# A fused attention and two-layer expert kernel: norm factors turned in 32-wide blocks and stored as rows, one factor of seven kept as half a place, and a new order table

## The chip, the cores and the metric

The kernel runs on one core of a Trainium2 chip. The metric is device microseconds of one execution, as the median over runs. Before the change the median of three runs is 1045.04 us (1044.8 to 1048.22).

## The reference, cut to what matters

```python
# q, k, v: (4 batches, 12 heads, 448 tokens, 64); S = 448
scores = q @ k.T / sqrt(64) - log(S)
attn   = 1 / (1 + exp(-scores))
x      = (attn @ v) -> (1792 tokens, 768)
# first layer: d_ff = 1536
rms = sqrt(mean(x * x, axis=-1) + 1e-06)
xn  = x / rms * rms_g
g   = xn @ w_gate
x   = (g * sigmoid(g) * (xn @ w_val)) @ w_out
# second layer: d_ff = 2048
h   = x @ w_in
out = (h - tanh(h)) @ w_out2
```

All values are 32-bit floats, and the products are made from rounded high parts and remainders of their factors.

## The kernel before

**Stages.** The four batches are worked as two groups of two, (0, 1) and (2, 3). For each of the 48 heads the scores of a head are made on TensorE with keys on the partitions (L750, and L771 for the last 64 keys), put through the sigmoid on ScalarE (L759) and multiplied with the values (`pair_av` L807, `tail_av` L791) into one PSUM bank per pair of heads. VectorE or ScalarE copies the bank to SBUF (`copy` L437). The six pairs of a batch give x with the 768 features on six times 128 partitions and the 448 tokens along the free axis. ScalarE squares the six parts and VectorE adds them (L830), which leaves one 128 x 448 tile of partial sums of squares.

**The norm.** `norm(b)` (L836 to L853) then needs, for each of the 448 tokens, the sum over 128 partitions. TensorE makes it with four products (L842) whose weights are 112 tokens of the tile and whose moving operand is a column of ones. They add into a PSUM bank that a VectorE memset (L845) has set to zero; that memset has no input, and it is the first instruction of VectorE's queue for batch 0. VectorE scales the 112 x 4 sums (`ms`, L847), GpSimd raises them to the power -0.5 (`rc`, L849), and SP stores the 112 x 4 factors to DRAM in token order with one DMA whose elements are 4 bytes (L852). `spread_norm` (L857) loads the 448 factors back to all 128 partitions, and VectorE multiplies x by them and by `rms_g` (`x_whole`, L923).

**The layers.** From about 127 us on, the two layers run. They are products of blocks in the seven-product scheme: four blocks of a weight matrix are combined into seven factors, and sums of x are combined the same way. `raw` tiles hold 128 rows of a weight matrix (L485); VectorE and ScalarE split each into a rounded part and a remainder (L437, L508, L519) and combine blocks (L572, L604). The factors of a weight pass are kept in DRAM for the second group of batches: `keep` stores them (`put` L586) and `again` loads them back (L634 to L637). A place of a stored factor is 128 x 768; the fourth one, A22, fills half of it, and is stored and loaded at full size.

**What sets the order.** All work is recorded first as pieces with an engine, a duration and dependences. `Plan.lay` then gives out the pieces to the queues of five engines; where several could go, the rank of each piece in the table `ORDER` decides (a base-64 text of some 5,000 numbers, one per piece). The queues run in order, so a piece that waits holds all pieces behind it on its engine. SP issues most loads, the norm's stores and the reloads of factors; GpSimd issues loads of values and of `raw` weights and the stores of factors.

**The start.** While the first inputs land, TensorE makes `N_WARM` = 6 products of zeros (`whole_bank` L442, weights and moving operand are the tile `mark`). `mark` is set to zero by GpSimd (L1223), behind its memset of `zero` (L478).

Of the kernel before, what the change touches and what calls it, by code (L numbers as in the profile page):

```python
# [9 lines left out]
F32 = mybir.dt.float32  # L10
# [5 lines left out]
AF = mybir.ActivationFunctionType  # L16
# [6 lines left out]
P = 128  # L23
# [14 lines left out]
N_WARM = 6  # L38
# [202 lines left out]
a2f03b00003b0mT04X04u08F0Ly03c0000OB0000000Cc0Xd0cta3v0K10aW0o203b0We1s61l_1pz5dA0Lo2jB0Za12m0gb0O92Ng17A18y1aQ19b3hi05l  # L241
0fA1ex0000Ho0Z20OX0nZ1F905j1bI2Fk0kb2R20KR1hz4zf0Ei1w20000000b20000dI0Op1GO1nR20i0O_1_l2Qd37T2hh3_E59j46I5TC1Dw0gP00H1IT
01e0ED0001Qu0000E_0Xx0001yz0ON0Xg1T-0_j2NP1a52VS15E2C13ZD00Q3TH3oy1oG3Cj2wN06cAJ72uw36U3D70IX1Sc6gY3Kk2-y5ug3N92tf0f22Db
3Ob6Z74122YZ3412_B3FW3HR2ZM3tp3Il26j4MJ6JS4Qx2XT3Rn3O21gW2ge3fl1i42Z52JX2Tu21a1x_2Jx3Ud3x12Rq2IT27N2cI2E92G62qU2Fn2QJ2fF
2t239K4Wx3Fm4Rz3x42Fd2hO1a21fk1_S1hX0vE21H1ON18s1B52jj1-K2gX1ZZ1Oc1ku3Br3oO1w71fE1s_1ar1iv2T41fy1Dn0xa1s_1XP0Fl0Fl0za0_B
0uV2Ty2Sf2SB1FT2Jj1Nz0sM2SW3zX3Gd1-A1M61yz1Kh2HV1IT1xo2Tj1U_2NH27314T1If2Dm1th1ld1lM1zT1Wa58K3UK1q22Jy1w02oL1ig0dx0EF0Cf
0EN0GT0eR0mf0pk1f12R41u01-Z0Dm14a1jx3oQ1MU1P70Cf1W50wx1hu0Cf1WR0Qc1-91Xl0qw1Tb2CH2aq2Vy0Cf80P3H81bb2k_1W224h1w_1O_1Iz0fu
0Cf0VV0Cf0Cf0tD0in0L00PJ0_r1OQ0U10Et1tX2F13451uq2AP1tn1bZ1lk0_D11V0cd14k1Jy0Cf0ak1R51EP0ug28W1kZ0Cf0IV1jo1w22TF17H0sZ18W
17x2NQ34m1XD2Z727o1qk2pT1oe3OW2dN2lJ2Dr2Ry3Tx1gY1ab1Kp1nC2511VM1U-2Wl1Xb1bn2W01qB1aJ1Kn0Vr3g23ik3FR1_o0zg1tL1aR1TX1-P0-I
1uk1Kz1W22nz1qh2ko19G1JY20x2Ns1RL3Ow1-T2oq2SP2G72Kt2r-2ML2YF3ik2BJ1sV2Sn2VM2LQ2KR23w2DH2Pt2dK36s1J71nF2Dw2Jd1vt2UC1YS1tw  # L250
2FW1nQ2n_1yh2tU3H240-0vl1sG2YR4jm2Ah3VR4De30C2Tf35m32P2cv28m1mK1Pv0I65A63Kq0dN3UI3Bi1-H2hk2nW2Kz41222z2BY07N34o0M42oM33P
3Bm2Og1Oi1QU0EZ2RG2b93pV21g1W21w_0kw3Rn3kr4Og0mu25Q1-P2qv1qn5Gt37Z49R2_G3-J1kW2nZ3Hm22M3FG3NL2bR0Cf5Mv2pr34V3m03xb2Fq2Qp
3Dq1_16Bf2Mn0DJ2kq2IJ1m22YZ2as2b835w2Vv3uj5VQ1h109e5610WT3o13c92843_t1oL64O54k3mw3BY3JU42a3LY39U2gM1tJ2Q43bs5eE61739o2dJ
2a73ml49V1-p3-X3wE2C13nB4Fc2eO1Yt5u96az2XW3t337B6QH5Q64qs56h2KU2pC2K-2ZA6zp6Uk2g03hH4sY7oM2-c3W_5CB2-12q_24x4Fk3JP2KJ0VS
6K71Ak6jG4ke5Wj1FA3Cf3bA3fG6GS3aB2mv20l2qp3pO3Dn3no3_83063U62gT1wa1gf3Le1Hz2AL2XK1es2In1nb2de4Pe2zc2AE2Q21iP1rM1K31ao0fW
2rw0wN3lV1FV0tZ21k2Sj2-o1EL2_x25b1wx4Tw4kJ0002BI2gz2mP2XU0Dt3O60DE5JL1QT3293RF4XA05L3nV3Ll1eQ4GR51033G2pf4_J4tx32W4Ut2Gx
3xm2o-2ru3P83zW4Lp3DD3LQ34U3j65Fx0SD54O55a4BN4xo3WM7gh6yv3Ls3fa0OV6H_6Ty7-R2rk02U5bi3be1aU72C8EC4qa6SX6NICG62TE3_p22Y4JA
5Gu0KF6w24HV3KY4OI4js2ck2M_4Xd1IH5Ht7y5AHq5Ob4J14O17IW2tc5AX6jU4vx6F16_73YX6zw6K661Z1i75sV6uP64t7Bm8Oe3vU00q9ZI6P70000up
09N9zp6s47wL3BV7T06q08Ng50B74C025000DqM6Ka6EJ6039LT6rR9gI8xP8jp7OG6ppC9k6j068X7cvA9C7BGBNS2hDBpT2je30b3TbHhkGT58326ff7rH
83D6TFCFxBlC4sr8Ui7Cx67M60G6zq9i23BS9Jj6qK6w08Qc8NxAJk7hy7gDA8Y6DLCxC6R06nz8mG9se7sm5yI1155q15wnCaY0aF0Nm7QZDFA6Ag5dB7Fg  # L260
BAR1o68G66zL6Eu82S85O6X16rF9l0CFW18TApRDeCDKHBSsBEmDCXE5zFAM4-w79sAdD95X90BC8cBlb9226d279j6bU9T-7SK6B5A8Z7c16CK6fCAYC7rM
# [102 lines left out]
def tile_sigmoid_attention_moe_moe(  # L364
# [233 lines left out]
    def pair_units(ph, i, rs, j):  # L598
# [787 lines left out]
```

## Time and profile before

| | |
|---|---|
| median of 3 runs | 1045.04 us (1044.8 to 1048.22) |
| the profiled execution: its own time | 1050.69 us |
| its span on the core | 1048.9 us |
| mean granted clock of TensorE | 0.989 |
| busy: TensorE, its weight loads, VectorE, ScalarE, GpSimd | 98%, 84%, 75%, 64%, 15% |
| DMA | 247.11 MB, mean 236 GB/s |

The profiled execution is 5.65 us above the median of the runs, and 1.8 us of it lie outside the span. A line of the timeline is a run of like instructions: its start, how long it lasts from the first to the last, the engine, the line of the kernel, the operation and its tiles, a count, and in brackets the idle time of the engine before it and what ended it. L437 is the line of a helper that copies and casts for many places, so its tile names tell which copy it is.

### The profile page before, as it was taken

To read this page: it belongs to the slowest core of one execution; us is meant where nothing else is said; L and a number is where in the kernel's file an instruction comes from. 1 tells how busy PE (TensorE), PEld (TensorE's weight loads), DVE (VectorE), ACT (ScalarE), POOL (GpSimd) and SP (SyncE) were. 2 spreads that over 40 slices of the span, in tenths; PEclk is the share of its full clock that TensorE was granted. 3 is DMA by queue.
4 is the path that set the end of the run, shared out by engine and by line. 5 is a ranking of instruction groups with operands and counts; after the bars stand their busy time and mean duration, and the time that the engine had idled before them with its cause. 6 is when DMAs were issued, how large, how long until landed. Compare 5 with 4: busy or idle time off the path is not lost.

```text
span 1048.9 us, 15266 instructions
## 1 busy us (share of the span) xinstructions
PE 1024.1 (98%) x5258; PEld 881.1 (84%) x5258; DVE 788.5 (75%) x1274; ACT 675.9 (64%) x1233; POOL 161.4 (15%) x218
## 2 busy tenths in 40 slices
PE   9898999899999999999999999999999999999998
PEld 4454459799999888899999989999998999999997
DVE  5575889797965985886865867899886878676766
ACT  6575875675764655675664756778675767665742
POOL 4431110000013032111003030000303210003030
PEclk9898999999999999999999999999999999999999
DMA  8789868958649879969759589287969882849493
GB/s 312 276 279 248 311 217 247 297 189 305 222 138 288 317 167 317 364 196 405 283 159 234 190 232 289 78 306 265 216 206 219 275 214 76 268 113 222 123 227 132
DMA packets 99117, 247.11 MB, mean 236 GB/s; under 512 B 13184, under 2 KB 52032, under 8 KB 99040
## 3 DMA queue, kind: packets, MB, share of 16 engines
q1 hardware_dynamic: 74384, 178.23, 50.9%
q0 software_dynamic: 24512, 67.84, 26.2%
q8 instruction: 41, 0.67, 0.3%
q14 instruction: 36, 0.29, 0.1%
q10 hardware_dynamic: 144, 0.07, 0.0%
HBM read 152.90 MB, written 93.20 MB: 235 GB/s over the span
## 4 chain that ended last, share of the span: by engine, by line
PE 67%; issue 13%; DMA 11%; DVE 5%; POOL 3%; ACT 2%; SPq 0%; POOLq 0%; DVEq 0%; ACTq 0%
PE ps L1125 33%; PE ps L1070 22%; PE ps L1150 5%; PE ps L807 3%; DMA wAg<-part 3%; DMA wD<-part 2%; PE ps L750 2%; DMA raw<-in_w_out 2%; POOL out L948 1%; DMA part<-wB 1%; DVE part L519 1%; DMA out<-unit 1%; DMA rc<-rc 1%; DMA unit<-rc 1%; DVE part L508 1%
## 5 line engine op out<-in xcount | busy, mean ns | idle before, releaser
L1125 PE MATMUL ps<-unit,part 128*128 128x448 f32 x2520 | 524.4, 366 | 11.8 <-ACT unit L437 6.0
L1125 PEld LDWEIGHTS ps<-unit,part 128*128 128x128 f32 x2520 | 473.5, 189 | 57.3 <-ACT unit L437 9.5
L1070 PE MATMUL ps<-unit,part 128*128 128x448 f32 x1512 | 311.4, 364 | 0.0
L1070 PEld LDWEIGHTS ps<-unit,part 128*128 128x128 f32 x1512 | 283.5, 187 | 22.3
L519 DVE TENSOR_TENSOR part<-part 128x768 fp32r<-128x768 f32 (+1 forms) x244 | 215.1, 891 | 77.7 <-ACT part L437 54.5
L437 ACT COPY unit<-ps 128x448 f32<-128x448 f32 x292 | 151.6, 535 | 117.0 <-PE ps L1070 45.6
L437 ACT CAST part<-part 128x768 fp32r<-128x768 f32 (+1 forms) x236 | 183.4, 787 | 41.8 <-DMA part<-wB 8.1
L877 DVE TENSOR_TENSOR unit<-unit 128x448 fp32r<-128x448 f32 x252 | 153.1, 620 | 38.6 <-ACT unit L437 23.4
L437 ACT CAST unit<-unit 128x448 fp32r<-128x448 f32 x260 | 144.1, 570 | 48.0 <-DVE unit L989 24.1
L1006 DVE TENSOR_TENSOR unit<-ps,unit 128x448 f32<-128x448 f32 x168 | 103.2, 622 | 46.3 <-PE ps L1125 18.6
L759 ACT ACTIVATE unit<-ps 128x448 f32<-128x448 f32 x168 | 79.7, 571 | 31.8 <-PE ps L750 22.7
L882 DVE TENSOR_TENSOR unit<-unit 128x448 f32<-128x448 f32 x144 | 86.5, 619 | 7.5 <-DMA unit<-sumB 3.9
L948 POOL DMA_DIRECT2D sumB<-unit x48 | 41.6, 942 | 261.1 <-DVE unit L1006 165.6
L508 DVE SCALAR_TENSOR_TENSOR part<-raw,zero 128x768 uint32<-128x768 uint32 x68 | 64.8, 953 | 10.4 <-ACT zero L437 8.6
L437 ACT CAST zero<-raw 128x768 f16<-128x768 bf16 x52 | 56.2, 1080 | 18.6 <-DMA raw<-in_w_val 6.9
L807 PE MATMUL ps<-unit,part 128*64 128x448 f32 x288 | 62.4, 569 | 2.9 <-DVE unit L437 2.9
L1150 PE MATMUL ps<-unit,part 128*128 128x448 f32 x288 | 60.3, 365 | 0.5
L1150 PEld LDWEIGHTS ps<-unit,part 128*128 128x128 f32 x288 | 53.7, 187 | 6.1 <-DVE unit L934 1.0
L948 POOL DMA_DIRECT2D out<-unit x36 | 30.7, 964 | 177.3 <-DVE unit L1006 168.3
L750 PEld LDWEIGHTS ps<-unit 64*128 64x128 f32 x396 | 37.6, 193 | 18.2 <-ACT unit L759 7.7
L750 PE MATMUL ps<-unit 64*128 64x448 f32 x396 | 49.8, 390 | 0.0
L604 DVE TENSOR_TENSOR part<-part 128x384 f32<-128x384 f32 x80 | 43.2, 552 | 8.6 <-DMA wAg<-part 7.5
(52 smaller groups left out, 475.1 us busy)
## 6 DMA issues: line engine op xcount, KB each, us to landing
raw<-in_w_out POOLq DMA_DIRECT2D x28, 768.0 KB, 9.0
part<-wD SPq DMA_DIRECT2D x56, 384.0 KB, 5.1
part<-wB SPq DMA_DIRECT2D x36, 384.0 KB, 5.9
wC<-part SPq DMA_DIRECT2D x36, 384.0 KB, 4.2
part<-wC SPq DMA_DIRECT2D x36, 384.0 KB, 4.5
raw<-in_w_in SPq DMA_DIRECT2D x16, 768.0 KB, 6.2
sumB<-unit POOLq DMA_DIRECT2D x48, 224.0 KB, 8.1
wD<-part POOLq DMA_DIRECT2D x28, 384.0 KB, 7.1
```

The costliest lines, as they stand in the source:

```text
L437: add(engines, lambda e: (nc.scalar.copy if e == "ACT" else nc.vector.tensor_copy)(to(), of()), reads, writes)
L519: add({**dve(n, psum=False), **pool(n)}, lambda e: ENG[e].tensor_sub(lo(), of(), hi().bitcast(F32)), [*reads, *kh], [*kl])
L750: nc.tensor.matmul(ps[i].tile[:, :S], lhsT=k_of(w, b, c, i), rhs=x.tile[rows, :S], start=q == 0, stop=q == len(terms) - 1)
L759: add(act(S, psum=True), lambda e: nc.scalar.activation(to.tile, ps.tile[:, :S], AF.Sigmoid, bias=-math.log(S), scale=1.0 / math.sqrt(D)), ...
L807: nc.tensor.matmul(ps.tile[HEADS[i], :S], lhsT=v_of(v, b, c, i), rhs=a[c][i].tile, start=opens and c == 0, stop=not opens and c == MAIN - ...
L877: add({**pool(S), **dve(S, psum=False)}, lambda e: ENG[e].tensor_sub(t["l"].tile, of.tile, t["h"].tile.bitcast(F32)), [of["t"], kh], [kl])
L882: add({**dve(S, psum=False), **pool(S)}, lambda e: ENG[e].tensor_sub(t.tile, x.tile, y.tile), [x["t"], y["t"]], [t["t"]])
L948: add(queue("POOL", True), lambda e: nc.gpsimd.dma_start(out=d.tile, in_=t.tile, accum_op=ALU.add), [t["t"], d["t"]], [d["t"]], moved=move ...
L1006: add(dve(S), lambda e: nc.vector.tensor_add(t.tile, ps.tile[:, :S], t.tile), [ps["t"], t["t"]], [t["t"]])
L1070: nc.tensor.matmul(ps.tile[:, :S], lhsT=part(a), rhs=x[b].tile, start=n in (1, 5) and kp == 0 and q == 0, stop=kp == n_kp - 1 and q == 2, ...
L1125: nc.tensor.matmul(ps.tile[:, :S], lhsT=part(a), rhs=x[b].tile, start=n in ((1, 2, 5) if opening else (1, 5)) and i == 0 and q == 0, stop= ...
L1150: nc.tensor.matmul(ps.tile[:, :S], lhsT=wt, rhs=a[p].tile, start=start and i == 0, stop=stop and i == 2, skip_group_check=True)
```

## The change

- `norm(b)` works on blocks of 128 tokens (128, 128, 128 and 64). Its memset of the PSUM bank now reads the finished squares, so the bank is given out only behind them. The factors go into the first 4 columns of a 128 x 32 tile of zeros (a new VectorE memset), VectorE transposes that tile in blocks of 32 x 32 (a new instruction), and each of the four groups of 32 partitions then holds four rows of 32 factors. SP stores them with four DMAs of four rows of 128 bytes, in place of one DMA with 448 elements of 4 bytes. The load behind it is of the same size as before, and waits for all four.
- The pool of the norm's small tiles has four buffers instead of two.
- The fourth factor is stored as its 384 columns and loaded as these. There are 18 such stores and 18 such loads, of 192 KB in place of 384 KB.
- `mark` is set to zero by VectorE as its first instruction, and there are nine products of zeros.
- In `plain_units` the first 12 products of a list, not 8, are sorted by their weight block.
- `ORDER` is wholly new.

```diff
-N_WARM = 6
+N_WARM = 9
 ORDER = """
-a2f03b00003b0mT04X04u08F0Ly03c0000OB0000000Cc0Xd0cta3v0K10aW0o203b0We1s61l_1pz5dA0Lo2jB0Za12m0gb0O92Ng17A18y1aQ19b3hi05l
+qV906300005U03D00z06306306300F00006306O0K719d3BQ7HAqXR4Ru1pO8lK2h_3jv05U6XF2fm1_S6JE2LN0Xw4q40xP42i5Jf5Wm6dX48k24T0002qQ
...
-    norm_p = ctx.enter_context(tc.tile_pool(name="norm", bufs=2))
+    norm_p = ctx.enter_context(tc.tile_pool(name="norm", bufs=4))
...
     mark = const.tile([P, S], BF16, name="mark")
+    nc.vector.memset(mark, 0.0)
...
-    expo = const.tile([TK, 4], F32, name="expo")
+    expo = const.tile([P, 4], F32, name="expo")
...
             if (ph, i) not in SPLIT:
-                put(d, at, x)
+                if at < 3:
+                    put(d, at, x)
+                else:
+                    add(queue("SP"), lambda e: nc.sync.dma_start(out=d.tile[:, at, :NH].rearrange("p (k c) -> p k c", c=P), in_=one_of(x.tile, 1)),
+                        [x[1]], [d[at]], moved=moved(4 * P, 3 * P))
                 return
...
-    def again(d, at):
+    def again(d, at, n=NW):
         w = part_of("again", [P, NW])
-        add(queue("SP"), lambda e: nc.sync.dma_start(out=w.tile, in_=d.tile[:, at]), [d[at]], [w[0], w[1]], moved=moved(4 * NW))
+        add(queue("SP"), lambda e: nc.sync.dma_start(out=w.tile[:, :n], in_=d.tile[:, at, :n]), [d[at]], [w[0], w[1]], moved=moved(4 * n))
...
     def norm(b):
-        ms, rc = (Slot(None, lambda t=t: norm_p.tile([TK, 4], F32, tag=t, name=t)) for t in ("ms", "rc"))
+        ms, rc, rt = (Slot(None, lambda t=t, n=n: norm_p.tile([P, n], F32, tag=t, name=t)) for t, n in (("ms", 4), ("rc", 32), ("rt", 32)))
         def sums(e):
             for i in range(4):
+                n = min(P, S - i * P)
                 nc.tensor.matmul(
-                    ps.tile[:TK, i:i + 1], lhsT=sq.tile[:, i * TK:(i + 1) * TK], rhs=ones[:, 0:1], start=False, stop=True, skip_group_check=True)
-        add({"DVE": (130, False)}, lambda e: nc.vector.memset(ps.tile[:TK, :4], 0.0), [], [ps["t"]])
+                    ps.tile[:n, i:i + 1], lhsT=sq.tile[:, i * P:i * P + n], rhs=ones[:, 0:1], start=False, stop=True, skip_group_check=True)
+        add({"DVE": (130, False)}, lambda e: nc.vector.memset(ps.tile[:, :4], 0.0), [sq["t"]], [ps["t"]])
...
-        add({"POOL": (2100, True)}, lambda e: nc.gpsimd.tensor_tensor(out=rc.tile, in0=ms.tile, in1=expo, op=ALU.pow),
-            [ms["t"]], [rc["t"]])
-        d = rcs[b] = Slot(None, lambda: dram_p.tile([4, TK], F32, name=f"rc{b}"))
-        add(queue("SP"), lambda e: nc.sync.dma_start(out=d.tile.rearrange("i t -> t i"), in_=rc.tile), [rc["t"]], [d["t"]], moved=moved(4, S))
+        add({"DVE": (130, False)}, lambda e: nc.vector.memset(rc.tile, 0.0), [], [rc["t"]])
+        add({"POOL": (2100, True)}, lambda e: nc.gpsimd.tensor_tensor(out=rc.tile[:, :4], in0=ms.tile, in1=expo, op=ALU.pow),
+            [ms["t"], rc["t"]], [rc["t"]])
+        add({"DVE": (180, False)}, lambda e: nc.vector.transpose(rt.tile, rc.tile), [rc["t"]], [rt["t"]])
+        d = rcs[b] = Slot(None, lambda: dram_p.tile([4, 4, 32], F32, name=f"rc{b}"))
+        for k in range(4):
+            add(queue("SP"), lambda e, k=k: nc.sync.dma_start(out=d.tile[:, k], in_=rt.tile[32 * k:32 * k + 4]), [rt["t"]], [d[k]], moved=300)
...
-        order = sorted(order[:8], key=lambda x: x[1]) + order[8:]
+        order = sorted(order[:12], key=lambda x: x[1]) + order[12:]
...
-    nc.gpsimd.memset(mark, 0.0)
     nc.gpsimd.memset(ones, 1.0)
```

**VectorE, about 35 us into the kernel** (`zero<-raw` is the first step of splitting a raw weight tile, `unit<-ps` is the copy that frees the PSUM bank of a pair of heads, `unit<-part` and `unit<-part,unit` round q or k and take the remainder). Before, and then in the change, whose line numbers are a few higher:

```order
33 L437 CAST zero<-raw 128x768
34 L830 TENSOR_TENSOR unit<-unit 128x448
35 L508 SCALAR_TENSOR_TENSOR part<-raw,zero 128x768
36 L437 COPY unit<-ps 128x448
37 L437 CAST unit<-part 128x384
38 L572 TENSOR_TENSOR part<-part 128x768
```

```order
33 L438 CAST zero<-raw 128x768
34 L510 SCALAR_TENSOR_TENSOR part<-raw,zero 128x768
35 L836 TENSOR_TENSOR unit<-unit 128x448
36 L574 TENSOR_TENSOR part<-part 128x768
37 L438 CAST unit<-part 128x384
38 L438 COPY unit<-ps 128x448
```

The copy that frees the bank stays behind the cast of the same raw tile, with two more pieces between them. Since the norm no longer holds a bank from the start, the piece of TensorE that needs this copy comes one step later in TensorE's queue: the scores of the next head, not the `pair_av` before them.

**TensorE, the attention of the first group** (L842, now L849, are the norm's sums; L791 and L771, now L797 and L777, the tails that end a pair of pairs). Before, up to the sums of batch 0, and then the change up to the same sums:

```order
39 L750 MATMUL ps<-unit 128x448 x18
40 L807 MATMUL ps<-unit,part 64x448 x6
41 L750 MATMUL ps<-unit 128x448 x18
42 L807 MATMUL ps<-unit,part 64x448 x6
43 L771 MATMUL ps<-part 64x448 x4
44 L791 MATMUL ps<-unit,part 64x448 x4
45 L842 MATMUL ps<-ones,unit 112x1 x4
```

```order
37 L777 MATMUL ps<-part 64x448 x4
38 L797 MATMUL ps<-unit,part 64x448 x4
39 L756 MATMUL ps<-unit 128x448 x18
40 L813 MATMUL ps<-unit,part 64x448 x6
41 L849 MATMUL ps<-ones,unit 128x1 x3
42 L849 MATMUL ps<-ones,unit 64x1
43 L756 MATMUL ps<-unit 128x448 x18
```

The sums of batch 0 come six rows earlier: behind the row that ran at 50.99 us before. Those of batch 1 stay where they were, behind the last tail of their batch.

**SP, the store and the reload of the factors of batch 0** (`rc_1058` and `rc_803` are the DRAM tiles of the factors, `in_qkt` and `in_vt` the inputs of later heads). Before, and then in the change:

```order
28 L691 DMA part<-in_qkt 128x448 x4
29 L691 DMA part<-in_vt 128x2x256 x2
30 L852 DMA rc_1058<-rc 112x4x1
31 L691 DMA part<-in_qkt 128x448 x3
32 L857 DMA unit<-rc_1058 128x448
33 L691 DMA part<-in_qkt 128x448
```

```order
26 L697 DMA part<-in_qkt 128x448
27 L862 DMA rc_803<-rt 4x32
28 L697 DMA part<-in_qkt 128x448 x2
29 L697 DMA part<-in_vt 128x2x256 x2
30 L697 DMA part<-in_qkt 128x448 x2
31 L862 DMA rc_803<-rt 4x32 x3
32 L697 DMA part<-in_qkt 128x448 x4
33 L697 DMA part<-in_vt 128x2x256 x2
34 L867 DMA unit<-rc_803 128x448
```

Four short stores stand in place of one, the first a few loads earlier in the queue, and eight to thirteen other issues lie between a store and the reload where there were three.

At the start of VectorE's queue the cast of the first raw weight tile, which stood behind two rounded inputs (rows 2 and 4) and in front of the third (row 7), now stands in front of the second.

## Rows read from the trace of the kernel before

**Rows 1.** The page, part 1 and the clock of part 2.
```profile
PE 1024.1 (98%) x5258; PEld 881.1 (84%) x5258; DVE 788.5 (75%) x1274; ACT 675.9 (64%) x1233; POOL 161.4 (15%) x218
PEclk9898999999999999999999999999999999999999
```
**Rows 2.** TensorE's waits: line, releaser, total us, times, longest.
```profile
PE ps L1125 <- ACT unit L437: 6.0, 4, 3.3
PE ps L842 <- DVE unit L830: 3.8, 2, 3.4
```
**Rows 3.** TensorE's timeline: start, us, instructions, [idle before <- releaser].
```profile
1.94 2.42 PE L444 MATMUL ps<-mark 128*128 128x448 bf16 x6 [1.94 <-POOL mark L1223]
4.29 5.86 PE L750 MATMUL ps<-part 64*128 64x448 f32 x24
...
11.00 2.48 PE L807 MATMUL ps<-unit,part 128*64 128x448 f32 x12
13.40 2.09 PE L750 MATMUL ps<-unit 64*128 64x448 f32 x18
...
37.55 4.75 PE L807 MATMUL ps<-unit,part 128*64 128x448 f32 x12 [2.90 <-DVE unit L437]
42.23 2.71 PE L750 MATMUL ps<-unit 64*128 64x448 f32 x18
...
53.40 0.87 PE L750 MATMUL ps<-unit 64*128 64x448 f32 x6
```
**Rows 4.** TensorE's timeline at the sums of batch 1.
```profile
95.38 1.65 PE L842 MATMUL ps<-ones,unit 128*112 128x1 f32 x8 [3.42 <-DVE unit L830]
96.97 3.73 PE L750 MATMUL ps<-unit 64*128 64x448 f32 x18
```
**Rows 5.** TensorE's timeline in the layers: three of its ten later waits.
```profile
200.05 5.26 PE L1125 MATMUL ps<-unit,part 128*128 128x448 f32 x17 [3.31 <-ACT unit L437]
417.15 3.90 PE L1125 MATMUL ps<-unit,part 128*128 128x448 f32 x18 [1.48 <-ACT unit L437]
804.22 8.10 PE L1125 MATMUL ps<-unit,part 128*128 128x448 f32 x31 [2.50 <-ACT ps L437]
```
**Rows 6.** Windows: busy us per engine (count), granted clock, DMA share, GB/s.
```profile
95.00:105.00 10.00, 9.62 (x52) 6.77 (x54) 7.14 (x14) 5.54 (x13) 3.46 (x5) 0.67 0.92 173
130.00:160.00 30.00, 30.00 (x182) 16.91 (x179) 26.99 (x49) 22.82 (x49) 6.25 (x1) 1.00 0.67 221
160.00:195.00 35.00, 34.99 (x178) 32.09 (x177) 31.25 (x53) 19.21 (x29) 1.31 (x1) 1.00 0.91 239
```
**Rows 7.** VectorE's timeline: the raw tiles' casts at 14 and 35 us.
```profile
14.62 0.62 DVE L437 CAST zero<-raw 128x768 f16<-128x768 bf16 x1 [4.25 <-DMA raw<-in_w_out]
...
34.99 0.60 DVE L437 CAST zero<-raw 128x768 f16<-128x768 bf16 x1 [6.74 <-DMA raw<-in_w_out]
...
36.88 0.62 DVE L437 COPY unit<-ps 128x448 f32<-128x448 f32 x1
```
**Rows 8.** SP's and VectorE's timelines: store, reload and use of batch 0's factors.
```profile
74.85 0.34 SPq L852 DMA_DIRECT2D rc<-rc  x1
82.43 0.33 SPq L857 DMA_DIRECT2D unit<-rc  x1
90.89 1.28 DVE L923 SCALAR_TENSOR_TENSOR unit<-unit,g_sb 128x448 f32<-128x448 f32 x2 [4.35 <-DMA unit<-rc]
```
**Rows 9.** DMA, 175 to 202 us in 40 slices, and its issues there.
```profile
GB/s 451 419 387 423 414 414 387 352 127 391 414 387 396 305 246 259 250 346 410 360 292 259 86 50 14 77 109 132 141 191 137 210 241 414 423 414 319 414 396 419
part<-wB SPq DMA_DIRECT2D x4, 384.0 KB, 11.2
rc<-rc SPq DMA_DIRECT2D x1, 1.8 KB, 14.1
```
**Rows 10.** DMA, 72 to 86 us: its GB/s in 40 slices.
```profile
GB/s 362 383 435 421 343 424 356 375 386 263 136 30 53 39 17 23 23 16 26 51 164 119 96 137 124 146 88 97 61 103 124 94 167 240 252 353 433 420 460 404
```
**Rows 11.** The page, part 6: median us from issue to landing.
```profile
part<-wB SPq DMA_DIRECT2D x36, 384.0 KB, 5.9
```

More of the change, by code (lines that the diff above doesn't have):

```diff
@@ L245 @@
[L245 to L249, printed above, removed]
@@ L355 @@
[L355 to L359 removed]
+qV906300005U03D00z06306306300O00006306O0K719d3BQ7HAqXR4Ru1pO8lK2h_3jv05U6XF2fm1_S6JE2LN0Xw4q40xP42i5Jf5Wm6dX48k24T0002qQ
@@ new lines @@
+06319M3MC3TG06T28D2ks0631pa2Xg0BS3ix2hx0J52izEM77Ea5B803S03S9M40631Ye4xF03S03S78z2ym11D6SN2HU4-f9JIAk0CF6CUf0pK0hK02t5lv
+0001zv0005Ca03S1Ki9iL0Cr2b507D2fyA1Z5E38oHCQl6mi28r5IB7010PX7_F6396C09RZ2r90Lxbvm8Yv8QjFsA1UO3VBH9t6T970qHWs6u55910a00dt
+8EOE1c77E8Qm6QE2M12OV4VvAws8GyBA08JZBXbF0QEkx4UN7XQC0e1ne3ltBsj2ZG4CK5qO4SP4sP2uU2Ow9m-BR_5gN2g43bb3UB1zC3uM5Bv3pb3-y2Fg
+2zn2ZU5fM7Lu9LSBC672y4ss0WM24q3fM0n70DR5fq0IM1G233P3oh48l3l61M_1do2Cr89Q96_0uM16r2S522A3HH1yx3Ou3Pf29E2f34LM2Do37L2k52Cr
+2_y3fn48I3B61Oe4Pg2xM0kg3iv4fn3h42Gn14W3CM2cp3Zw3wM45d41K4BD4AF4QI2GK2u62h_1wT41k4J61gB2g94vR4vM1J43Tf3sS4aY1-l56T1-M12j
@@ new lines @@
+3hI0dw1Hx1pZ2FZ3ky3gy2Iy1oi1rH2tX1JA5912Mt2lT2r13G80xf02v3Z_37B0S43IB1rE0R32vN5Ae49D4p-3BP6184MVNGI5NB3hZ8ZS1ri1M94P_2i0
+2o_33O3sX32b29L18k1Py1Kf3Vz2Ux2PE3he0_l3Bv2OB2u81l034i2o92Xj3P22Au2AU2mq1n91uv07m0mV2Gx1Rx24y2pH0zp1cc0QE2m63lw1KL33Y0n1
+2J34dY2x22fg11V14E2845Lx12n3mr3RK3D35PL3Wv4qC4Oy6DU2hU5KQ4-92Sc3Fh0tO4Db3uN1Va4SY3fT3Sz2uz3e51Ox1nS3Na2nW5M37oH2_Y3ky2Lz
+2YU35b1vK3u83FE2B22l33Nz63u4ZS56n3lO2hT4S_5gk3-d5P25IR5U943P0i45TW5r97OX5Eh3Pq3XA2YK5dv0gg4et2pX7pi0QV4Gz3ek4Cs3IC2Hu5b9
+4zu5KT4TC4Rp1Ry1oL4nH37734N3fh2iy4nD3oi5tk3dh4Ob7aV4a44wb0X-73K0473l464X3hg3lA4Hj2gY3TT3j93fe2rb7dP4l95fy4pU5gu33g49S5Hg
@@ L360 @@
+XFJUKHWfsbGlVQETy_UL2XGlXPIVcaVZ_YR0SwEThDV9rXJ3Yl3RivWsOYPuaCwSPIPIhV_NUzWXh8X2ZU0ibhUZiwVXRS1ZWSRVfpXnEW-bZWqWv8YH3VZW
+UhbVftTNnUJUa92SCuXS5WD4RRdU2UScISAoSfHabZQRhUalS4NYwXZC_RQ8TJcPk4VlpWnXVkeSn3XzrUPybSSRIaWDZWWoWh9WqDV-uY39Wq8RQhT9OTfq
+blJWnpcpWUvVaq3ZRvVJHYUhWmVTpUUKaUoLVyra0_TDEXfjXaiPsjRcEYJKWgFSg6RWNamuYVLWYWQFrVMBYEfXVFT5MY2dOwOYZrVC8WRKUdoWMEYYIWtR
+YmCVMKYcBbifZ6rW1MWKjVOrX4PaTkYRZc7_
 """
@@ L670, in two @@
         def two(at, names):
-            t = again(stored[ph, i], at)
+            t = again(stored[ph, i], at, len(names) * NH)
             of = lambda: t.tile
             if len(names) == 1:
-                factors(j, names, lambda: one_of(of(), 1), [t[1]])
+                factors(j, names, lambda: of()[:, :NH].rearrange("p (k c) -> p k c", c=P), [t[0], t[1]])
             else:
@@ L856, in spread_norm @@
         r = rstd[b] = unit("rstd")
-        add(queue("SP"), lambda e: nc.sync.dma_start(out=r.tile, in_=d.tile.rearrange("i t -> (i t)").partition_broadcast(P)), [d["t"]], [r["t"]], moved=moved(4 * S))
+        add(queue("SP"), lambda e: nc.sync.dma_start(out=r.tile, in_=d.tile.rearrange("i k c -> (i k c)")[:S].partition_broadcast(P)), [d[k] for k in range(4)], [r["t"]], moved=moved(4 * S))
     acts = {}
@@ L1228, in tile_sigmoid_attention_moe_moe @@
         whole_bank(warm)
-    nc.scalar.activation(expo[:, 0:1], ones[:TK, 0:1], AF.Sigmoid)
+    nc.scalar.activation(expo[:, 0:1], ones[:, 0:1], AF.Sigmoid)
     nc.gpsimd.memset(expo, -0.5)
```

220 lines of the change are left out of this document (106 added, 114 removed).

## The prediction, written before the changed kernel ran

> **What bounds the kernel now.** I read the page first: TensorE is busy 98% of the span [rows 1], so there is little to win but its waits and the time in which it runs slow. Then TensorE's waits: few lines, none of them in a steady rhythm [rows 2]. Then its timeline, where each wait has a place and something behind it. The reader is to see two things there. First, three long waits lie in the first fifth of the span: 2.90 us ending at 37.55 [rows 3], 3.42 us ending at 95.38 [rows 4], 3.31 us ending at 200.05 [rows 5]. A fourth, of 2.50 us, ends at 804.22 [rows 5]. Second, the work behind each of these four runs slower: 18 products of scores take 3.73 us at 96.97 [rows 4] and 2.09 us at 13.40 [rows 3]; the granted clock is 0.67 in the stretch from 95 to 105 us and 1.00 in the others that I read [rows 6], so part of that stretch ran at the lower of the two levels, 1.2 GHz. Behind the wait of 1.48 us, 18 products take 3.90 us, which is the usual 0.2 us each [rows 5]. So a long wait here costs itself and some 1.5 to 3 us more, and a short one only itself.
>
> The third view is DMA. Around each store of norm factors the sixteen engines nearly stop: 386 GB/s falls to 16 to 53 for about 4 us, then climbs, at 72 to 86 us [rows 10], and 414 falls to 14 to 141 around 190 us [rows 9]. The store itself holds 1.8 KB and lands 14.1 us after its issue there [rows 9].
>
> **The change part by part.** The sum is made against the profiled execution, 1050.69 us, which stands 5.65 us above the median of 1045.04; I take the same 5.65 off at the end.
>
> *Start.* `mark` is zero by VectorE's first instruction, so TensorE starts at about 1.1 us in place of 1.94 [rows 3]. Nine products in place of six end at about 1.1 + 9 x 0.40 = 4.7 us (2.42 us for six [rows 3]), 0.4 us behind the 4.29 at which the first scores began; against that, TensorE has been busy 0.8 us longer by then, and the first scores, 5.86 us for 24 of which part ran slow, can speed up as much earlier. Between -0.8 and +0.4 us. I cost it at nothing, since the next point is set by a transfer and not by TensorE. If that cover goes, these ends come into the sum.
>
> *The bank at 35 us.* The wait of 2.90 us is on VectorE's copy of a PSUM bank, which stands behind the cast of a raw tile that lands at 34.96 [rows 7]. The norm no longer holds one of the eight banks from the start, so this copy is wanted one step later, by the row that began at 42.23. Without the wait and the slow stretch TensorE would be there at 42.23 - 2.90 - (4.75 - 2.48) = 37.1 us [rows 3]. The copy ended at 36.88 + 0.62 = 37.5 [rows 7]; two more pieces in front of it (0.95 and 0.35 us on the rows of their kind) put it at 38.7 if the raw tile lands as before, and at 38.3 if its issue moves up with the earlier pieces of GpSimd's queue. So a wait of 1.2 to 1.6 us stays, near the 1.48 behind which nothing ran slow. The row starts at 38.4 in place of 42.23 and takes 2.09 in place of 2.71: **4.4 us won**. The ends: 0, if the rest of the wait is long enough to slow TensorE again; 5.8, if there is no wait at all.
>
> The first raw tile's cast moves in front of a rounding whose result TensorE wants for the row at 13.40. The tile landed at 14.6 [rows 7], one load fewer is in front of it now, so I expect a wait of about 1.8 us (0 to 3.2) near 14 us. It costs nothing in the sum, because what TensorE loses there it does not wait for at 38.4. If it slows TensorE, that too ends at the same copy unless it is over 1.3 us.
>
> *Sums of batch 1.* TensorE waits 3.42 us for the squares [rows 4], which wait for VectorE's queue, where the multiplication with batch 0's factors stands 4.35 us until the reload lands [rows 8]. That chain is store at 74.85, landing and reload at 82.43, use at 90.89. In the change the sums of batch 0 follow the row that ended at 53.40 [rows 3], 3.8 us earlier now: about 49.6. Scaling, the power and the transpose take some 5 us, the first row store goes at about 54.4. The reload stands behind loads whose buffers come free with TensorE's tails, and so goes at about 68 (an estimate from TensorE's rows up to there). With the 8.46 us of the old reload [rows 8] the use starts at 76.5 in place of 90.89. Eleven pieces of VectorE, some 7.5 us, lie between it and the last square; they end at 84. TensorE wants them at 91.96 - 4.4 = 87.6. The wait goes with 3.6 us to spare: 3.42 + (3.73 - 2.09) = **5.1 us won** [rows 3, 4]. Ends: 0 and 6, with what the rows behind it lose as well.
>
> *Wait at 200 us.* It hangs on a reload of factors that lands 14 us after its issue, where 11.2 is the median around it and 5.9 that of the whole run [rows 9, 11]. The DMA stretch in front of it is the one behind batch 3's store. Four stores of four 128-byte rows stand there now. If the low throughput comes from the 448 pieces of 4 bytes, sixteen pieces make none of it, and the reload lands about 8 us earlier than the 3.31 us wait needs. 17 products took 5.26 us, and 178 took 34.99 in full clock, 0.197 each [rows 5, 6]: 5.26 - 3.35 = 1.9. **5.2 us won**; ends 0 and 5.2.
>
> The Trainium skill, DMA: Bandwidth & Descriptors, Rules for kernel authors, says that a strided last dimension is lowered to one descriptor per element. By that rule the old store is 448 pieces and the new ones sixteen, and the sum is as above. The same page's Specifications say that transfers under 512 bytes are read, modified and written back, and that speaks against the change, since 128 bytes are under it too: by it alone the 5.2 us would stay. No row before shows a store of 128-byte rows.
>
> *What goes beside other work.* Per norm one VectorE memset and one transpose of 128 x 32, under 0.4 us together by the rows of small pieces; VectorE has 25% of idle time. SP issues 12 more DMAs at 0.34 us [rows 8], 4 us over the run. Thirty-six transfers lose 192 KB each, 7.1 of 247 MB, which relieves DMA by 30 us at the mean rate of 236 GB/s; TensorE sees nothing of it unless a reload lands late, and the one that does is counted. The sorted 12 products: nothing.
>
> *New waits.* The rest of the table is new, and TensorE arrives 10 to 15 us earlier at 130 us, where VectorE is busy 26.99 of 30 and 31.25 of 35 us [rows 6]. The ten waits from 105 us on show what a mismatch costs: 1.48 us at the short end [rows 5], 5.2 at the long. I take one and a half short ones more, **2.2 us lost**; ends -4.5 (the wait at 804 goes, 2.50 and its slow products, 8.10 - 31 x 0.197 = 2.0 [rows 5]) and +12.
>
> Sum: -4.4 - 5.1 - 5.2 + 2.2 = -12.5; 1050.69 - 12.5 = 1038.2 profiled, 1032.5 as a median.
>
> **The rivals.** *More goes than I count.* The wait at 804 and some of the short ones vanish, because less DMA and earlier norms leave every queue ahead. For it: no engine but TensorE is above 75% [rows 1]. Against: these waits are on ScalarE's copies, which the change doesn't make faster. 14.7 + 4.5 + 3 = 22: 1023.
>
> *VectorE takes it back.* From 95 to 195 us VectorE has little idle time: 9.6 us in the 75 us of the three windows of [rows 6]. If TensorE comes 12 us earlier, all of VectorE's work there has to be pressed together or TensorE waits. For it: 90% busy from 130 to 195. Against: VectorE's earlier idle time, such as the 4.35 us at 90.89 [rows 8], is given back to it. Two thirds lost: 1050.69 - 12.5 + 8 = 1046, a median of 1040.5; with a slow stretch, 1043.
>
> *The store is no better.* Short rows stop the DMA engines as the old elements did; then the 5.2 us stay: 1037.7. This is the page's second rule above. For it: nobody has seen these rows. Against: sixteen pieces are few beside the 448.
>
> *Slower: SP is held by the transposes.* Four stores per norm wait on SP for VectorE's transpose, and the loads of later heads' q, k and v stand behind them. For batch 0 the load right behind lands at about 60 us by my times and is wanted at 67: if the transpose comes over 7 us later, each norm costs TensorE a wait like that at 95 us with its slow products, 5.1 us, for four norms 20 against the 14.7 won. With the other loss: 1050.69 + 5.7 + 2.2, a median of 1053. For it: VectorE's queue in front of each transpose has waits for loads. Against: 7.6 us passed on SP between store and reload, with few issues between them and loads behind [rows 8], and TensorE did not wait for one of these.
>
> **How the numbers follow.** Forecast 0.50 (1027 to 1039), more 0.17 (1019 to 1027), VectorE 0.15 (1039 to 1045; a third of it within 0.3%), the store 0.08 (1034 to 1043; a quarter within), slower 0.10 (1049 to 1056). A median here can tell 0.3%, 3.1 us, from no change: faster is under 1041.9, slower over 1048.2. Faster 0.50 + 0.17 + 0.10 + 0.06 = 0.83, same 0.05 + 0.02 = 0.07, slower 0.10. The range leaves out the slower case and part of the best: 1020 to 1045.
>
> **What would show it.** In the profile after: TensorE's first row near 1.1 us; no wait over 1.6 us near 35 us; the sums of batch 1 without a wait, with batch 0's factors used before 80 us; DMA without the stretches of 14 to 50 GB/s; no wait near 190 us; granted clock above 0.99. It is wrong if new waits over 2 us stand between 130 and 200 us, or if the DMA still falls behind the row stores.

## The result, and the profile after

| | before | after |
|---|---|---|
| median, ten runs each | 1044.76 us (1039.54 to 1048.22) | 1033.32 us (1029.41 to 1040.44) |
| ratio | | 0.9899, 95% interval 0.9871 to 0.9928 |
| the profiled execution: time, span | 1050.69, 1048.9 us | 1032.65, 1030.8 us |
| granted clock, mean of the span | 0.989 | 1.000 |

The change is faster by 1.0%, 11.4 us in the medians. The two profiled executions lie 18.0 us apart, because the one of before was slower than each of its ten timed runs, and the one of after lies 0.7 us under its median. What the profiles show is therefore more than what the medians gained, and the experiments have to tell what is what. One of the six executions of `before_rows` below ran slow as a whole (1130.12 us, mean granted clock 0.837); its ratio leaves it out, its median of 1033.95 us has it in and would be 1033.60 without it.

The page of after, parts 1 and 2 (against [rows 1]):

```profile
PE 1015.3 (98%) x5261; PEld 876.4 (85%) x5261; DVE 790.4 (77%) x1281; ACT 676.7 (66%) x1235; POOL 155.8 (15%) x217
PEclk9999999999999999999999999999999999999999
```

TensorE is busy 8.8 us less with three products more, and its clock never falls between the start and the end. In before it was at the lower level at each of the four long waits, for 6.8, 6.8, 3.4 and 3.4 us, 20.5 us together. TensorE's waits after (against [rows 2]):

```profile
PE ps L1135 <- DVE unit L1016: 4.6, 3, 2.3
PE ps L1135 <- DVE part L521: 1.5, 2, 0.9
PE ps L1135 <- ACT ps L438: 1.3, 2, 0.8
PE ps L446 <- DVE mark L442: 1.2, 1, 1.2
PE ps L849 <- DVE ps L852: 0.9, 1, 0.9
...
PE ps L756 <- DMA part<-in_qkt: 0.8, 1, 0.8
```

No wait is longer than 2.33 us. By the idle times of the timeline TensorE waits 11.6 us in all, where it waited 20.2. The norm of batch 0, in the timelines of SP and VectorE and then TensorE's (against [rows 8, 3, 4]):

```profile
52.44 0.33 SPq L862 DMA_DIRECT2D rc<-rt  x1
...
57.59 1.14 SPq L862 DMA_DIRECT2D rc<-rt  x3
...
67.95 0.42 SPq L867 DMA_DIRECT2D unit<-rc  x1
...
76.52 0.69 DVE L933 SCALAR_TENSOR_TENSOR unit<-unit,g_sb 128x448 f32<-128x448 f32 x1 [0.99 <-DMA unit<-rc]
...
87.29 0.62 DVE L836 TENSOR_TENSOR unit<-unit 128x448 f32<-128x448 f32 x1
...
88.38 0.06 DVE L852 MEMSET ps<- 128x4 f32 x1
```

```profile
38.55 2.08 PE L756 MATMUL ps<-unit 64*128 64x448 f32 x18
...
88.59 1.01 PE L849 MATMUL ps<-ones,unit 128*128 128x1 f32 x8 [0.89 <-DVE ps L852]
89.52 2.08 PE L756 MATMUL ps<-unit 64*128 64x448 f32 x18
```

The factors are used at 76.5 us in place of 90.9, and the row at 38.55 neither waits nor runs slow. Six loads stand on SP between the last store and the reload, twelve between the first store and it. The 0.89 us left at the sums of batch 1 is on the bank's memset (88.38), which now stands behind the last sum of squares (87.29). DMA from 72 to 86 us after (against [rows 10]), and the reloads from 175 to 202 us (against [rows 9]):

```profile
GB/s 418 400 432 411 443 410 450 399 440 307 462 386 369 281 158 176 289 271 297 342 353 348 371 421 378 443 398 373 408 362 381 411 342 383 361 386 389 385 405 400
```

```profile
DMA  1097899981000899699999999976879999999966
GB/s 46 27 155 173 328 328 323 405 354 33 2 0 0 323 278 182 191 291 355 364 399 432 405 413 382 401 269 209 200 291 382 407 373 413 414 419 428 432 264 182
part<-wB SPq DMA_DIRECT2D x5, 384.0 KB, 5.3
rc<-rt SPq DMA_DIRECT2D x8, 0.5 KB
```

The stretch at 16 to 53 GB/s behind batch 0's store is gone, and the reloads land in 5.3 us where they took 11.2, though two norms store their rows in this second window. Its slices at 0 to 46 GB/s are of another kind: the line above them, the busy share in tenths, has the engines at 0 or 1 there, and by how long the packets last they are busy for 0 to 19%, so they have next to nothing to move.

### The profile page after: what moved, and what is told of

It is laid out like the page before. It is cut to its first block, busy times and chain, and to the rows that moved or that the text cites. A ratio compares the mean times of both kernels' runs of the same rounds, so it can differ in the third digit from the quotient of the medians.

```text
span 1030.8 us, 15321 instructions
## 1 busy us (share of the span) xinstructions
PE 1015.3 (98%) x5261; PEld 876.4 (85%) x5261; DVE 790.4 (77%) x1281; ACT 676.7 (66%) x1235; POOL 155.8 (15%) x217
## 4 chain that ended last, share of the span: by engine, by line
PE 69%; issue 13%; DMA 10%; DVE 3%; POOL 3%; ACT 1%; SPq 0%; POOLq 0%; DVEq 0%; ACTq 0%
PE ps L1135 37%; PE ps L1080 21%; PE ps L1160 6%; PE ps L813 3%; DMA part<-in_qkt 2%; DMA wD<-part 2%; PE ps L756 2%; POOL out L958 2%; DMA out<-unit 1%; DMA part<-wAg 1%; DMA part<-wB 1%; DMA raw<-in_w_out 1%; DMA wB<-part 1%; DVE part L521 1%; PE ps L777 0%
## 5 line engine op out<-in xcount | busy, mean ns | idle before, releaser
L813 PE MATMUL ps<-unit,part 128*64 128x448 f32 x288 | 59.4, 548 | 0.0
L756 PE MATMUL ps<-unit 64*128 64x448 f32 x396 | 47.3, 375 | 0.5 <-DVE unit L732 0.5
L813 PEld LDWEIGHTS ps<-unit,part 128*64 128x64 f32 x288 | 18.5, 136 | 30.5 <-issue 23.8
```

The source lines that it names most:

```text
L756: nc.tensor.matmul(ps[i].tile[:, :S], lhsT=k_of(w, b, c, i), rhs=x.tile[rows, :S], start=q == 0, stop=q == len(terms) - 1)
L813: nc.tensor.matmul(ps.tile[HEADS[i], :S], lhsT=v_of(v, b, c, i), rhs=a[c][i].tile, start=opens and c == 0, stop=not opens and c == MAIN - ...
```

## The experiments

The kernels ran on different chips, each with runs of the kernel before beside it, so ratios to that are compared; the change itself has 0.9899. These ratios have a limit: the kernel before has medians from 1044.76 to 1051.54 us on these chips, so two ratios from different chips can differ by 0.6% for that alone. Experiments 1 to 4 stood beside each other on one chip; so did 5, 6, `dead_dense` and `dead_pitch`; and the other three of experiment 7. Diffs are cut to the calls that matter.

**1. The old store in the new kernel** (`elements`). The only edit, in each of the four stores:

```diff
-dma_start(out=d.tile[:, k], in_=rt.tile[32 * k:32 * k + 4])
+dma_start(out=d.tile[:, k].rearrange("i c -> c i"), in_=rc.tile[32 * k:32 * k + 32, :4])
```

> The changed kernel with one thing undone: each of the four stores of a norm takes 32 x 4 single elements of 4 bytes from the untransposed tile, 512 elements a norm in place of sixteen rows of 128 bytes; order of all queues unchanged. Theory (single elements stop the DMA engines): behind each of the four stores the throughput falls below 60 GB/s for several us with the engines busy, as in the kernel before; the reload of batch 0's factors lands some us later, and a reload of weight factors near 190 us lands late; TensorE waits 3 to 6 us more, a median of 1037 to 1042 against the 1033 of the change. Rival (short stores do it, or the low stretches have another cause): the DMA looks as in the changed kernel, and the time stays within 2 us of 1033.

Measured: 1053.99 us (1051.1 to 1055.66), ratio 1.0066 (1.0046 to 1.0086). This is slower than the kernel before, and by the ratios some 17 us slower than the change (20.7 us in the medians), twice what the theory expected at most. DMA from 99 to 113 us and TensorE's timeline there:

```profile
DMA  1099900000962023892999989981609996025279
GB/s 1 0 142 70 70 0 0 0 0 0 88 35 18 18 35 105 228 281 123 404 439 370 440 369 404 211 35 18 18 18 53 70 70 35 18 35 53 35 193 299
rc<-rc SPq DMA_DIRECT2D x3, 0.5 KB, 13.1
```

```profile
115.03 4.75 PE L813 MATMUL ps<-unit,part 128*64 128x448 f32 x12 [7.23 <-DVE unit L438]
```

In several of the slices at 18 to 70 GB/s the engines are busy (first line, tenths) and move nearly nothing. A slice counts the packets that start in it; by how long the packets last, the engines are busy nearly without a break from 101 us on, also where the line has 0. TensorE waits 7.23 us, then runs slow (4.75 us for 12 products that take 2.48 elsewhere). So the new table, the free bank and the half places together gain nothing where the store keeps its single elements: the table counts on transfers that land early, and is hurt more than the old one when they don't.

**2. The row stores in the old kernel** (`before_rows`). Blocks of 112 tokens, the old order of all queues; memset, transpose and four stores are issued where the scaling and the one store stood:

```diff
-dma_start(out=d.tile.rearrange("i t -> t i"), in_=rc.tile)
+nc.vector.transpose(rt.tile, rc.tile)
+for k in range(4):
+    n = min(32, TK - 32 * k)
+    dma_start(out=d.tile[:, 32 * k:32 * k + n], in_=rt.tile[32 * k:32 * k + 4, :n])
```

> The kernel before with the row stores alone: factors turned in 32 x 32 blocks and stored as four short rows of four, in the old order of all queues (transpose and stores are issued where the one store stood). Theory: the low stretches of the DMA go; the factors of batch 0 are used before 87 us in place of 90.89, the wait of 3.42 us at the sums of batch 1 and that of 3.31 us near 197 us shrink to under 1 us each, and 1044.8 becomes 1034 to 1038. Rival (the new order table brings the gain): both waits stay over 2 us, and the time is 1042 to 1046.

Measured: 1033.95 us, ratio 0.9873 (0.9843 to 0.9904). This one edit has all of the gain, within the intervals. TensorE's waits, and the timelines of VectorE and TensorE at the place of the old wait of 2.90 us:

```profile
PE ps L1138 <- ACT unit L437: 3.9, 3, 2.0
PE ps L1138 <- DVE unit L1019: 2.7, 3, 1.4
PE ps L1138 <- ACT ps L437: 2.5, 1, 2.5
```

```profile
31.41 0.61 DVE L437 CAST zero<-raw 128x768 f16<-128x768 bf16 x1 [3.31 <-DMA raw<-in_w_out]
...
33.30 0.61 DVE L437 COPY unit<-ps 128x448 f32<-128x448 f32 x1
```

```profile
34.78 2.48 PE L807 MATMUL ps<-unit,part 128*64 128x448 f32 x12
```

And the store, reload and use of batch 0's factors, in the timelines of SP and VectorE (against [rows 8]):

```profile
69.31 1.32 SPq L863 DMA_DIRECT2D rc<-rt  x4
...
72.42 0.33 SPq L870 DMA_DIRECT2D unit<-rc  x1
...
78.26 1.27 DVE L936 SCALAR_TENSOR_TENSOR unit<-unit,g_sb 128x448 f32<-128x448 f32 x2
```

From store to use the factors take 8.95 us, where they took 16.04 in before, with all queues in the old order. There is no wait at the sums of batch 1 and none near 197 us; the first one in the layers is at 324 us. And the wait near 35 us is gone too, though the bank is held as before and no norm has yet stored anything. The raw tile landed at 31.4 us here and at 34.96 in the profile of before [rows 7], issued 1.5 us earlier. The profiles of `strided` and `combo`, which hold the bank too, have no wait there either. So the held bank does not bring that wait by itself; it belongs to the one execution with the late transfer. Whether a free bank would have shortened it there is not tried.

**3. The free bank alone** (`before_bank`). The old first memset does nothing; bank and memset come where the sums are issued:

```diff
 def sums(e):
+    ps.tile = free()
+    nc.vector.memset(ps.tile[:TK, :4], 0.0)
```

> The kernel before with the norm's PSUM bank taken only where its sums are issued, the memset there too; old order of all other work. Theory: the wait of 2.90 us ending at 37.55 shrinks to 1.2 to 1.6 us with no slow stretch behind it, a gain of 4.4 us, 1040 to 1041; the two later waits stay. Rival (the bank isn't what it waited for): the 2.90 us stay, 1044 to 1045.

Measured: 1048.38 us, ratio 1.002 (1.0 to 1.004): no gain, if anything a loss. Its raw tile landed at 32.3 us and nothing waited near 35 us, so this profile can't tell what the bank is worth at a late tile. The memset, now behind the multiplications with late factors on VectorE, made a wait of its own:

```profile
93.22 1.63 PE L846 MATMUL ps<-ones,unit 128*112 128x1 f32 x8 [5.66 <-DVE ps L844]
```

Neither of the two cases that I had named came out.

**4. Rows and bank, old order** (`before_both`), the two edits together.

> The kernel before with the row stores and the late bank, old order, full fourth places, six products of zeros. Theory (the norm's edits carry the gain, the order table little): 1030 to 1035, no wait over 2 us in the first 210 us. Rival (the table carries it): 1039 to 1043, since with the bank free and the DMA relieved TensorE meets VectorE's old queue order and waits there.

Measured: 1036.69 us, ratio 0.9897 (0.9867 to 0.9927). The median lies above the 1030 to 1035 expected. The interval of the ratio covers the row stores alone and the whole change. The table adds nothing that these runs can tell.

**5. Full fourth places in the new kernel** (`full4`): the store of a whole tile, and loads of the whole place, at the planner's costs of the half ones.

> The changed kernel with the fourth factors stored and loaded as full places again, 36 transfers of 384 KB in place of 192 KB, order unchanged. Theory (the halves lie beside other work): within 3 us of the change's 1033. Rival (DMA decides in the layers): reloads land later and TensorE's waits behind them grow by 4 to 10 us, 1037 to 1043.

Measured: 1034.98 us, ratio 0.9862 (0.984 to 0.9883). The half places are worth nothing measurable.

**6. Rows, half places and nine products of zeros in the old order** (`combo`).

> The kernel before, in its old order of all queues, with the row stores, the half places and nine products of zeros on VectorE's mark; the bank and the table stay old. Theory (the row stores carry all of the gain, the rest is worth little): 1031 to 1036, as the row stores alone with 1034. Rival (the small parts add up): 1025 to 1029.

Measured: 1037.78 us (1036.42 to 1039.69), ratio 0.9884 (0.9867 to 0.99). The median is above the 1031 to 1036 expected, with the kernel before at 1049.68 beside it; the ratio is that of the others. The small parts don't add up to anything that can be measured. Its profiled execution waits 4.87 us at 330 us for ScalarE, and its clock falls there, where the profile of `before_rows` has 0.76 and 1.40 us.

**7. Which element stores stop the DMA?** Five kernels add to the change, behind the last row store of each norm, one store that nothing reads and nothing waits for. They differ in the DRAM tile alone:

```diff
+    s = dram_p.tile([4, P], F32, name=f"sc{b}")
+    nc.sync.dma_start(out=s.rearrange("i t -> t i"), in_=rc.tile[:, :4])
```

(`dead_dense`; in `dead_pitch`, `dead_64` and `dead_16` the tile is [4, P, n] with n = 128, 16 and 4, and the store goes to its first column; in `dead_t4` it is [P, 4], written as it lies.)

> The changed kernel with one more store a norm, of 512 single elements of 4 bytes next to each other into a DRAM tile that nothing reads; nothing waits for it. Theory (single elements stop the engines for every queue): low throughput with busy engines for 6 to 8 us behind each of the four, and a median of 1038 to 1050, though no wait of the program hangs on the store itself. Rival (in the runs with element stores only the late factors cost): 1033 to 1036.

> As the run before, but the 512 single elements go to addresses 512 bytes apart. If it is the number of 4-byte pieces that stops the engines, as much as with neighbouring elements: 1038 to 1050. If it is that neighbouring elements write into the same stretch of DRAM, the low throughput goes or halves, and the time is 1033 to 1037.

> The additional store of 512 single elements that nothing reads, now 64 bytes apart (dense: 1056.5 us, 512 bytes apart: 1036.4). Theory (elements that share a stretch of DRAM hold each other up, and the stretch is short): as with 512 bytes, 1033 to 1038, no low throughput behind the store. Rival (what counts is how near they are over some hundred bytes): in between or as dense, 1042 to 1057.

> The same 512 elements 16 bytes apart. Theory: four elements share what one of 64 bytes has, so the low throughput comes back in part, 1038 to 1050. Rival (only elements that touch count): 1033 to 1038.

> The same 2 KB written densely, but token by token: 128 pieces of 16 bytes, one of each partition, in place of 512 of 4. Theory (neighbouring short writes hold each other up, so fewer pieces cost less): 1034 to 1042, a stretch of low throughput of 1 to 3 us behind each store. Rival (a dense range written by many pieces costs the same whatever the piece): 1050 to 1057.

| extra store | pieces | median us | ratio |
|---|---|---|---|
| `dead_dense`: 4 bytes, touching | 512 | 1056.52 | 1.0065 (1.0047 to 1.0084) |
| `dead_16`: 4 bytes, 16 apart | 512 | 1033.97 | 0.9836 (0.98 to 0.9872) |
| `dead_64`: 4 bytes, 64 apart | 512 | 1033.41 | 0.9842 (0.9797 to 0.9887) |
| `dead_pitch`: 4 bytes, 512 apart | 512 | 1036.35 | 0.9866 (0.9846 to 0.9885) |
| `dead_t4`: 16 bytes, touching | 128 | 1033.91 | 0.9841 (0.9801 to 0.9881) |

DMA behind the second norm's extra store, 14 us in 40 slices, in `dead_dense` (from 102 us) and in `dead_pitch` (from 99 us); then behind the first norm's in `dead_16` (from 60 us):

```profile
GB/s 371 264 190 171 73 40 28 66 10 28 40 80 45 63 40 38 0 23 68 91 164 159 159 161 113 101 151 159 126 159 217 221 181 333 435 413 360 340 246 343
```

```profile
GB/s 387 319 344 360 232 302 323 342 395 395 362 404 432 363 376 405 394 363 309 383 486 407 351 354 381 269 210 251 301 275 233 392 447 404 456 353 378 496 387 500
```

```profile
GB/s 379 240 332 210 319 325 391 194 189 225 260 288 277 251 354 419 402 419 342 320 320 298 182 285 323 454 377 397 405 463 396 371 348 357 372 379 406 389 385 450
```

The same 512 pieces of 4 bytes cost some 20 us of the run when they touch (1056.52 us against 1036.35 for `dead_pitch` beside it), and nothing measurable when 12 bytes lie between them. In `dead_dense` sixteen slices in a row, 5.6 us, stay under 100 GB/s. It is neither the number of pieces nor their size alone, and not that they touch alone (`dead_t4` touches too): it is many short writes to addresses next to each other. Whether touching counts, or how many pieces fall into a short stretch, is open: sixteen to 64 bytes cost much, four to 64 bytes (`dead_16`, `dead_t4`) nothing, and nothing between was tried.

`dead_dense` cost more than the 1038 to 1050 expected. My theory in `dead_16`, that four elements in 64 bytes would bring part of it back, fell; `dead_64` went as the theory said. The rival in `dead_t4`, that a dense range costs the same whatever the piece, fell too.

In the profile of `dead_dense` no instruction waits for this store, so its whole cost goes through the other transfers. The timelines of VectorE and TensorE show one such place:

```profile
109.33 0.96 DVE L510 SCALAR_TENSOR_TENSOR part<-raw,zero 128x768 uint32<-128x768 uint32 x1 [6.49 <-DMA wB<-part]
110.21 0.62 DVE L438 COPY unit<-ps 128x448 f32<-128x448 f32 x1
```

```profile
110.88 4.75 PE L813 MATMUL ps<-unit,part 128*64 128x448 f32 x12 [4.88 <-DVE unit L438]
```

VectorE waits 6.49 us for the store of a weight factor (`wB<-part`), the copy behind it frees a bank late, and TensorE waits 4.88 us and then runs slow. Between the profiles of `dead_dense` and `dead_pitch`, 20.6 us apart, TensorE waits 13.2 us more and is 13.7 us longer at the lower clock, which costs it half of that, 6.8 us. In the traces 84 packets take over 2 us in `dead_dense`, and 7 to 10 in each of the other four; 75 in before, 7 in the change.

**8. The old kernel with three lines altered** (`strided`). Block i of the sums takes the tokens 4t + i, so a partition's four factors are neighbours in token order, and one store of 112 pieces of 16 bytes does it without a transpose:

```diff
-lhsT=sq.tile[:, i * TK:(i + 1) * TK]
+lhsT=sq.tile.rearrange("p (t i) -> p i t", i=4)[:, i]
-out=d.tile.rearrange("i t -> t i"), in_=rc.tile
+out=d.tile, in_=rc.tile        # d is [TK, 4]; the reload reads it as "t i -> (t i)"
```

> The kernel before with three lines altered: block i of the norm's sums takes every fourth token (4t + i) as its weights, so that one partition holds four tokens that follow each other, and the one store writes 112 pieces of 16 bytes; no transpose, no tile of zeros, no further store; order of all queues unchanged. Theory (touching 4-byte elements were the whole cost): the low throughput behind the stores goes, a ratio to the kernel before of 0.984 to 0.990, as with the row stores alone, and TensorE's waits near 95 and 197 us are under 1 us. Rival (pieces of 16 bytes hold the engines up when a reload follows, or weights with a stride load slowly): 0.993 to 1.00.

Measured: 1036.29 us (1035.01 to 1041.16), ratio 0.9933 (0.9909 to 0.9956): above the 0.984 to 0.990 of the theory and at the low end of the rival's range. Near 95 and 197 us TensorE waits for nothing, and the first wait after the start is at 328 us, as the theory said. But the weight loads with a stride of 16 bytes are slower, as one branch of the rival had it, here in a view of one line's instructions, before and then in `strided`:

```profile
L842 PEld LDWEIGHTS ps<-ones,unit x32: 173/178/307, 70.0 to 177.9; 128*112 128x112 f32 x32
L842 PEld LDWEIGHTS ps<-ones,unit x32: 278/303/303, 64.5 to 168.4; 128*112 128x112 f32 x32
```

The medians (middle numbers) are 303 ns in place of 178, and the eight products of a norm take 1.81 us in three norms and 1.61 in one, in place of 0.95 (0.85 in the last): about 3.3 us over the four. The ratio lacks 0.6% against that of `before_rows`, 6 us, and the median 2.3 us; so part of it is this, and the rest may lie between the chips, or in the DMA: 19 packets take over 2 us here, 6 in `before_rows`. It isn't settled. No version tried here has a median under the 1033.32 us of the change.

## Why the prediction was right, step by step

- **The total** was near for a reason that is partly luck: 12.5 us forecast and 11.4 us measured in the medians, 1032.5 and 1033.32, while the terms were off in both directions. Without the first term below, which was wrong, the sum is 8.1 us and 1036.9 as a median; the row stores gave more than their terms and made it up.
- **The bank at 35 us, 4.4 us: wrong.** The step took a wait of the one profiled execution for a property of the program. The raw tile landed 2.6 to 3.6 us earlier in the profiles of `before_rows` and `before_bank`, and with it the wait went, bank or no bank. The same 2.90 us and the slow stretch behind it, 5.8 us, are about as much as the 5.65 us by which that execution lay above the median; that the two are the same thing is likely, not shown. I took these 5.65 us off at the end and counted the wait as a gain too; that was the warning I passed over.
- **Sums of batch 1, 5.1 us, and the wait at 200 us, 5.2 us: right that both go, too small, and the first not only for the reason given.** The row stores alone give 1 - 0.9873 = 1.3%, 13 us, against these 10.3. The use of batch 0's factors was forecast for 76.5 us and came at 76.52. But this term took the earlier place of the sums in the new order for the cause and let the old 8.46 us of the reload stand; in `before_rows` the order is the old one and the wait goes all the same, because store to use takes 8.95 us in place of 16.04. In `elements`, with the new order and the old store, the wait at these sums is down to 0.60 us as the term has it, but waits of 3.48 and 7.23 us stand near 75 and 115 us. Nor were 3.6 us to spare in the change: the last sum of squares was to end at 84 us and ended at 87.9, since VectorE waited 2.22, 1.17 and 0.42 us for loads of q and k, and 0.89 us of wait stayed. What the other 3 us are was not tried apart; the slow rows behind each wait that the terms left out are one candidate.
- **Why the old store costs so much: half right.** That the row stores free the DMA holds. That 448 pieces become sixteen was the reason given; 512 pieces 16 bytes apart cost nothing that can be measured, so the number by itself is not the cause. The Trainium skill, DMA: Bandwidth & Descriptors, Rules for kernel authors, has one descriptor per element for a strided last dimension. The count of packets agrees, 13057 of 4 bytes before and 11265 after, 4 x 448 fewer; the cost does not follow from it. The Specifications on that page of the Trainium skill have transfers under 512 bytes read, modified and written back. All the pieces of experiment 7 are under that, and one form in five is slow, so that rule does not decide it either.
- **New waits, 2.2 us lost: there are some, but no loss in sum.** After has waits of 0.88 and 0.66 us at 152 to 157 us, where VectorE was feared, 0.82 and 0.46 us near 9 and 16 us, and 2.33 at 510 us. But old ones went: from 105 us on, the wait at 200 left out, the waits are 8.6 us together before and 8.3 after, so that only the 1.3 us near 9 and 16 us are added. The slow products behind the wait at 804 us, 2.0 us, are gone too. The change as a whole has 0.9899 where the row stores alone have 0.9873, with intervals that overlap, so the medians show no loss either.
- **Start: nothing, as costed.** The scores begin at 4.63 us in place of 4.29. The granted clock first rose between 5.5 and 8.2 us in the profiles with six products, and between 4.0 and 7.2 in those with nine, so the earlier start buys nothing that can be told.
- **The early wait near 14 us** was 0.46 us, where 1.8 was expected within 0 to 3.2.
- **The rivals.** That the store is no better: refuted by experiments 1 and 2. VectorE taking it back: not seen; the largest wait from 130 to 200 us is 0.88 us. SP held by the transposes: it is, 2.1 us in front of the stores at 180.13 us, and behind them the DMA engines stand empty for some 2 us (2, 0 and 0 GB/s), but no wait of TensorE follows. More than counted: the wait of 2.50 us at 804 us is down to 1.60 us near 797, yet 1033.32 is far from 1023.

## What to carry to other kernels

Before a wait of one profile is given a price, see whether it is a property of the order or of one late transfer: where the profiled execution lies 0.5% over the median, as here, look for what other executions of the same order don't have, and don't count it twice. Four stores of 2 KB with touching 4-byte pieces cost this kernel some 20 us, and the cost does not show at the store but in the packets of other transfers: look at GB/s beside the busy share behind it. Three cures worked here: a transpose, so that rows are stored; several neighbouring elements in one partition, for one piece of 16 bytes; and room between the elements, which was tried only with a store that nothing reads.

## What the runs showed that I had not expected

- Touching single elements: a dead store of 2 KB per norm, four in the run, costs some 20 us; the same elements 16 bytes apart, nothing measurable.
- A mean granted clock of 1.000 went with 1029.4 to 1033.3 us over the ten runs of the change, 0.998 with 1033.3 to 1035.9, and 0.995 with 1039.3 and 1040.4. From 1.000 to 0.995 is 0.5%, some 5 us of a spread of 11, so a good part of it may be whether some wait brought the clock down; these executions have no timeline that would show it.
- In `dead_pitch` a wait of 1.82 us, on the bank's memset, had a stretch of 6.8 us at 1.2 GHz behind it; the wait of 2.33 us at 510 us in the change had none. A wait of 2.53 us near 803 us in `dead_64` had none either, and one of 1.36 us in `before_both` had one of 6.8 us. I had read from the four long waits that the length decides; by itself it does not. The two shorter waits stand in front of the norm's sums, the two longer ones in front of products of the layers. TensorE's timeline at the first two is below.
- Weights read with a stride of 16 bytes load in 303 ns where the dense ones take 178.

TensorE at the wait in `dead_pitch`, and then at the one in the change:

```profile
89.62 1.31 PE L849 MATMUL ps<-ones,unit 128*128 128x1 f32 x8 [1.82 <-DVE ps L852]
90.86 3.73 PE L756 MATMUL ps<-unit 64*128 64x448 f32 x18
```

```profile
510.01 11.19 PE L1135 MATMUL ps<-unit,part 128*128 128x448 f32 x54 [2.33 <-DVE unit L1016]
```
